# Routing attention and an MLP mixer on one core: six chunks of scores in one run, then six of values

## The chip, the core and the metric

The kernel runs on one core of one Trainium2 chip. The metric is the device time of one execution in microseconds (us). Three runs of the kernel before gave 885.87, 886.28 and 886.34 us; the median is 886.28. The profile shown is of one further execution, whose run took 886.28 us, and whose first and last profiled instructions lie 884.2 us apart: that distance is called the span below.

## What is computed

There are 4 batches and 8 heads, each with 768 queries, 768 keys and values of depth 64. Every query and key is assigned to the centroid it is most similar to (16 per head), and a query attends only to the keys with its own centroid. The outputs of the heads, side by side, are the 768 x 512 input of a mixer.

```python
q_assign = np.argmax(np.einsum('bhsd,hcd->bhsc', q_n, c_n), axis=-1)
k_assign = np.argmax(np.einsum('bhsd,hcd->bhsc', k_n, c_n), axis=-1)
scores = scale * np.matmul(q, k.transpose(0, 1, 3, 2))
scores = np.where(q_assign[..., :, None] == k_assign[..., None, :], scores, -1e9)
attn = softmax(scores)
x = (attn @ v), heads side by side
h = np.maximum(x.transpose(0, 2, 1) @ w_tok1, 0.0) @ w_tok2
u = x + h.transpose(0, 2, 1)
out = u + np.maximum(u @ w_ch1, 0.0) @ w_ch2
```

## The kernel before, in words

**Pairs and chunks.** The attention handles two heads at a time: 16 pairs g (4 batches x 4), one after the other. The 768 keys are six chunks of 128 (`NJ = 6`), the 768 queries two halves `qh` of 384 (`HS`). One chunk for one half of the queries is the smallest piece of work: 12 of them in a pair, 192 in all. The scores of a chunk lie with the keys on the partitions, and for both heads, in one tile `sc` of 2 x 512 fp32[...]. The pool `ps_sc` has three such tiles.

- **Scores (L430).** For each of the two heads a bf16 matmul of the one-hot rows of the centroids (`ohT`), which gives a large negative number wherever the centroids differ, and then a fp32 matmul of keys and queries (`T`, shown as `qkT`). The heads lie on partitions 0 to 63 and 64 to 127, so each matmul uses 64 rows of the array. A fp32 matmul is two instructions in the trace.
- **Exponential (L436).** ScalarE (ACT) turns one `sc` tile into a tile `ex` of 128 x 768, of which there are six (pool `work`).
- **Values (L461).** For each head `va` times `ex`, into 64 columns of the array, summed over the six chunks in the one tile `av`; ACT copies it to `avT` (L469).
- **Sums (L447, L451).** VectorE (DVE) adds the six `ex` of a half up. This gives the denominators.

**Small steps of a pair.** `load(g)` (L132) issues nine DMAs on SyncE's queue (SP). `turn(g)` (L284) transposes the queries and keys on DVE in blocks. `route_products` (L298) multiplies them with the centroids; `route` (L308), `route_big` (L337) and `route_count` (L330, on ACT) find the centroids and mark them; `route_turn` (L339) transposes the marks with a DMA. `pair_sums` (L478), `pair_denominators` (L482) and `pair_reciprocals` (L485) treat the denominators of the pair before, `half_turn` (L491) transposes its `avT`, and `half_out` (L499) divides and stores. Two tiles named `small` and `px`, for L298, L478 and L491, come from the same three tiles of `ps_sc`.

**Rounding of the weights.** `weight_steps` (L177) loads pieces of the mixer's weights and rounds them: per step three DVE operations, two ACT operations and a DMA. There are two steps in each of the first six pairs (`EARLY`), then one.

**Order.** The order on each engine is the order in which the code issues, since the kernel is built with a manual schedule. L816 loops over groups `m` of three chunks, four groups to a pair. In each turn it issues the sums of group m-1, the scores of group m and the values of group m-1: values follow one group late. The small steps hang on `s`, the group's number within its pair. `scores` issues the bf16 matmuls of two chunks, the fp32 ones of these two, and then those of the third chunk.

**Begin and end.** `begin` (L764) handles pair 0 apart: `turn_first` (L367) transposes on TensorE into a tile `pt`, whose two halves (queries, keys) are copied out by ACT (L790) and DVE (L791); L793 (ACT) and L279 (DVE) copy the centroids out of `pc`; L395 (ACT) and L393 (DVE) copy the marks out of `po`. After the last group come the token products (`tok1` L526, `tok2` L537), in their midst the small steps of the last pair (L857), and then the channel products, 525 us of the span.

Of the kernel before, what the change touches and what calls it, by code (L numbers as in the profile page):

```python
# [8 lines left out]
F32 = mybir.dt.float32  # L9
# [3 lines left out]
ALU = mybir.AluOpType  # L13
ACT = mybir.ActivationFunctionType
AX = mybir.AxisListType

B, H, S, D = 4, 8, 768, 64
C = 16
P = 128
NJ = S // P  # L20
DM = H * D
# [9 lines left out]
QP = P // NQ  # L31
NPAIR = B * NF

NG = 3
GROUPS = 2 * NJ // NG
EARLY = 6
SM_SCALE = 0.125

# [9 lines left out]
def kernel(  # L48
# [35 lines left out]
    def pool(name, bufs, stack=None, **kw):  # L84
        return (stack or fast).enter_context(
            tc.tile_pool(name=name, bufs=bufs, reuse_waits="tile", **kw)
        )
# [1 line left out]
    ps_w = pool("ps_w", 1, space=PSUM)  # L89
    ps_av = pool("ps_av", 1, space=PSUM)  # L90
    ps_sc_stack = fast.enter_context(ExitStack())
    ps_sc = pool("ps_sc", NG, ps_sc_stack, space=PSUM)

    xpool = pool("xpool", 1)
    wc1pool = pool("wc1pool", 1)
# [268 lines left out]
                    )  # L364
        nc.sync.dma_start(st["va"], v[0, 0:2].rearrange("h (p j) d -> p h j d", p=P))

    def turn_first(n):  # L367
        st = state[0]
        pt = ps_sc.tile([P, 2, 512], F32, tag="sc", name="pt")
        js = slice(HJ * n, HJ * n + HJ)  # L370
        for a in (1, 0):
            for j in range(HJ):
                nc.tensor.transpose(
                    out=pt[:, a, j * P : (j + 1) * P],
                    in_=st["rows"][:, n, a, j].rearrange("p h d -> p (h d)"), identity=ident,
                )
        return [
            (st["T"][:, a, js].rearrange("p j t -> p (j t)"), pt[:, a, 0:HS]) for a in range(2)
        ]

    def route_turn_first(n):
        po = ps_w.tile([P, 2, HJ, P], BF16, tag="w", name="po")
# [7 lines left out]
    def route_first_out(n, po, a):  # L390
        out = state[0]["ohT"][:, a, HJ * n : HJ * n + HJ]
        if a == 0:
            nc.vector.tensor_scalar_mul(out=out, in0=po[:, 0], scalar1=-BIG)  # L393
        elif n == 0:
            nc.scalar.copy(out=out, in_=po[:, 1])  # L395
        else:
            nc.vector.tensor_copy(out=out, in_=po[:, 1])

    def second_first():

        po = route_turn_first(1)
        for a in (1, 0):
            route_first_out(1, po, a)
        for n in range(2):
            route_count(0, slice(HJ * n, HJ * n + HJ), NPAIR * n)
        nc.vector.tensor_tensor(
            out=cells[:, 0:1], in0=cells[:, 0:1], in1=cells[:, NPAIR : NPAIR + 1], op=ALU.add
        )
        state[0].pop("rows")


    def split(m):

        g, s = divmod(m, GROUPS)
        return g, s // (GROUPS // 2), NG * (s % (GROUPS // 2))

    def scores(m):
        g, qh, j0 = split(m)
        st = state[g]
        js = slice(HJ * qh, HJ * qh + HJ)  # L420
        scs = [ps_sc.tile([P, 2, 512], F32, tag="sc", name="sc") for _ in range(NG)]

        for chunks in (range(NG - 1), (NG - 1,)):
            if m == 0 and len(chunks) == 1:
                second_first()
            for src, start in ((st["ohT"], True), (st["T"], False)):
                for i in chunks:
                    for h in range(2):
                        rows = slice(h * D, (h + 1) * D)
                        nc.tensor.matmul(  # L430
                            scs[i][:, h, 0:HS], lhsT=src[rows, 1, j0 + i], rhs=src[rows, 0, js],
                            start=start, stop=not start,
                        )
        for i in range(NG):
            ex = work.tile([P, 2, HS], F32, name="ex")
            nc.scalar.activation(out=ex, in_=scs[i][:, :, 0:HS], func=ACT.Exp, scale=SM_SCALE)  # L436
            st["ex", qh, j0 + i] = ex

    def add_up(m):
        g, qh, j0 = split(m)  # L440
        st = state[g]
        e = [st["ex", qh, j0 + i] for i in range(NG)]
        if j0 == 0:
            if qh == 0:
                st["sum"] = sums.tile([P, 2, 2, HS], F32, name="sum")
            acc = st["sum"][:, qh]
            nc.vector.tensor_tensor(out=acc, in0=e[0], in1=e[1], op=ALU.add)  # L447
            e = e[2:]
        acc = st["sum"][:, qh]
        for ex in e:  # L450
            nc.vector.tensor_tensor(out=acc, in0=acc, in1=ex, op=ALU.add)  # L451

    def values(m):
        g, qh, j0 = split(m)
        st = state[g]
        if j0 == 0:
            st["av"] = ps_av.tile([P, HS], F32, name="av")
        for j in range(j0, j0 + NG):
            ex = st.pop(("ex", qh, j))
            for h in range(2):  # L460
                nc.tensor.matmul(  # L461
                    st["av"][h * D : (h + 1) * D], lhsT=st["va"][:, h, j], rhs=ex[:, h],
                    start=(j == 0), stop=(j == NJ - 1),
                )
        if j0 == NJ - NG:
            if qh == 0:
                st["avT"] = sums.tile([P, NJ, P], F32, name="avT")
            js = slice(HJ * qh, HJ * qh + HJ)
            nc.scalar.copy(out=st["avT"][:, js].rearrange("p j t -> p (j t)"), in_=st.pop("av"))  # L469

    def pair_sums(g, den):

# [291 lines left out]
    def begin():  # L764
# [21 lines left out]
        keep_warm(12)  # L786
        pc = centroids_norm(cen)
        keep_warm(2)
        tq, tk = turn_first(0)
        nc.scalar.copy(out=tq[0], in_=tq[1])  # L790
        nc.vector.tensor_copy(out=tk[0], in_=tk[1])  # L791
        centroids_out(pc)
        nc.scalar.copy(out=cnT, in_=pc)  # L793
        keep_warm(2)
        pr = ps_sc.tile([P, 2, 512], F32, tag="sc", name="pr")
        route_products(0, pr[:, 0, 0 : HS // 2], js[0])
        for out, src in turn_first(1):
            nc.scalar.copy(out=out, in_=src)
        route(0, js[0])
        keep_warm(2)  # L800
        po = route_turn_first(0)
        for a in (1, 0):
            route_first_out(0, po, a)
# [2 lines left out]

    begin()
    weights = list(weight_steps(stage, W, ("tok1", "tok2", "ch1")))
    last = NPAIR * GROUPS
    ends = [lambda t=t: tok1(0, t) for t in range(NT)]  # L810
    for b in range(B):
        if b + 1 < B:
            ends += [lambda b=b, t=t: tok1(b + 1, t) for t in range(NT)]
        ends += [lambda b=b, j=j: tok2(b, j) for j in range(NJ)]

    for m in range(last + 3):  # L816
        g, s = divmod(m, GROUPS)
        more = g < NPAIR - 1
        old = g - 1 if m < last else -1
        if s == 2:  # L820
            if old >= 0:
                pair_denominators(old)
            if more:
                route(g + 1)
                route_big(g + 1)
                route_count(g + 1)
            if old >= 0:
                pair_reciprocals(old)
        if s == 3 and old >= 0:
            for qh in range(2):  # L830
                half_out(old, qh)
        if more and s == 0 and m > 0:
            turn(g + 1)
        if 1 <= m <= last:
            add_up(m - 1)
        if m < last:
            scores(m)
        if m == 0:
            turn(1)
        if 1 <= m <= last:  # L840
            values(m - 1)
        if m < last and s == 1:
            two = ps_sc.tile([P, 2, 512], F32, tag="sc", name="small")
            if old >= 0:
                pair_sums(old, two[:, 0, 0:HS])
            if more:
                route_products(g + 1, two[:, 1, 0:HS])
        if more and s == 2:
            route_turn(g + 1)
        if m < last and s == 2 and old >= 0:  # L850
            two = ps_sc.tile([P, 2, 512], F32, tag="sc", name="px")
            for qh in range(2):
                half_turn(old, qh, two[:, qh, 0:HS])
        if m == last:
            ps_sc_stack.close()
            pools["ps_m"] = pool("ps_m", 2, space=PSUM)
        if m == last + 1:  # L857
            pair_sums(NPAIR - 1, ps_w.tile([P, HS], F32, tag="w", name="den"))
            pair_denominators(NPAIR - 1)
            pair_reciprocals(NPAIR - 1)  # L860
            half_turn(NPAIR - 1, 0, ps_w.tile([P, HS], F32, tag="w", name="px"))
            half_turn(NPAIR - 1, 1, ps_av.tile([P, HS], F32, name="av"))
        if m == last + 2:
            for qh in range(2):
                half_out(NPAIR - 1, qh)
        if s == 1 and g + 2 < NPAIR:
            load(g + 2)
        if m == last - GROUPS:
            assert not weights
            routing.close()  # L870
            W["ch2"] = pool("wc2pool", 1, side="right").tile([P, NCT, DM], F32, name="wc2")
            weights = list(weight_steps(stage, W, ("ch2",)))
        if m < last - GROUPS:

            n = s == 1 or s == 3 and g < EARLY
        else:
            n = m % 2 if m < last else 2
        for _ in range(min(n, len(weights))):
            weights.pop(0)()
        if m >= last:  # L880
            for _ in range(3):
                ends.pop(0)()
    assert not state
    attention.close()
    pools["wsums"] = pool("wsums", 1, side="right")
# [239 lines left out]
```

## Time and profile before

| engine | busy us | share of the span | what it does most |
|---|---|---|---|
| PE (TensorE, matmuls) | 869.9 | 98% | L430, L461, later L662 and L713 |
| PEld (TensorE, loads of the stationary operand) | 519.0 | 59% | beside PE |
| DVE (VectorE) | 492.1 | 56% | L451 |
| ACT (ScalarE) | 289.3 | 33% | L436 |
| POOL (GpSimd) | 42.2 | 5% | rounding |

The DMA engines are busy for 22.6% of the span on the main queue. The clock granted to TensorE is 0.997 of full speed on the mean. A row of a group says: line, engine, operation, output and inputs, shapes and count, then busy time in us and the mean duration of one in ns, then how long the engine was idle ahead of the group and who ended that. A row of the timeline says: start in us, time until the last of the merged instructions ends, engine, line, operation and count. "PE busy" counts to a modelled end of each matmul, so that two matmuls in a row overlap in the record, and a pause shorter than that overlap isn't seen as idle.

### The profile page before, as it was taken

The page shows a single profiled execution, that of the slowest core. Times are in us where ns is not written, and L with a number is a line of the kernel's source. Part 1 is how long each engine was busy: PE and PEld are TensorE (multiplying, and loading weights), DVE is VectorE, ACT ScalarE, POOL GpSimd, SP SyncE. Part 2 cuts the span into 40 slices and gives each one's busy share as a digit, 9 for nine tenths or more (in the row PEclk, how much of TensorE's full clock was granted, in tenths as well). Part 3 has the DMA queues.
Part 4 walks back from the last instruction along what each step waited for, and adds up shares of the span by engine and source line. Part 5 has one row for each costly group of instructions (what it writes and reads, how often), then busy time and mean ns, then how long its engine had stood idle before and what let it go on. Part 6 is the DMA issues. An engine that isn't in the chain of part 4 may idle for free.

```text
span 884.2 us, 11022 instructions
## 1 busy us (share of the span) xinstructions
PE 869.9 (98%) x4293; PEld 519.0 (59%) x4293; DVE 492.1 (56%) x847; ACT 289.3 (33%) x507; POOL 42.2 (5%) x40
## 2 busy tenths in 40 slices
PE   8999999999999999999999999999999999999996
PEld 4444444444444444444568587686776867768675
DVE  5788888777777765695463334433344333343342
ACT  3665665555555454221120311203113021120210
POOL 1010011000010001230000000000000000000000
PEclk9999999999999999999999999999999999999998
DMA  8655665444554121220000001000010000100001
GB/s 159 148 121 118 140 131 112 100 96 97 106 120 80 19 91 47 85 82 1 0 1 1 0 29 44 0 1 1 24 48 1 0 1 25 47 1 1 0 25 50
DMA packets 133275, 47.61 MB, mean 54 GB/s; under 512 B 122080, under 2 KB 126176, under 8 KB 133216
## 3 DMA queue, kind: packets, MB, share of 16 engines
q1 hardware_dynamic: 131616, 46.45, 22.6%
q8 instruction: 35, 0.57, 0.3%
q10 hardware_dynamic: 1600, 0.39, 0.2%
q14 instruction: 24, 0.20, 0.1%
HBM read 34.64 MB, written 6.29 MB: 46 GB/s over the span
## 4 chain that ended last, share of the span: by engine, by line
PE 97%; DVE 1%; ACT 1%; DMA 0%; issue 0%; DVEq 0%
PE sc L430 18%; PE av L461 15%; PE pX L713 14%; PE pX L662 14%; PE pZ L713 7%; PE pZ L662 7%; PE ph L531 5%; PE pu L540 5%; PE pY L713 4%; PE pY L662 4%; PE px L491 1%; PE small L478 1%; PE pt L603 1%; PE small L298 1%; ACT uT L606 0%; DMA cen<-in_centroids_dram 0%
## 5 line engine op out<-in xcount | busy, mean ns | idle before, releaser
L436 ACT ACTIVATE ex<-sc 128x768 f32<-128x768 f32 x192 | 143.8, 807 | 63.3 <-PE sc L430 46.8
L430 PE MATMUL sc<-qkT 64*128 64x384 f32 x768 | 144.7, 482 | 0.0
L461 PE MATMUL av<-ex,va 128*64 128x384 f32 x768 | 137.8, 494 | 0.0
L451 DVE TENSOR_TENSOR sum<-sum,ex 128x768 f32<-128x768 f32 x128 | 121.1, 946 | 10.6 <-DVE sum L447 0.5
L461 PEld LDWEIGHTS av<-ex,va 128*64 128x64 f32 x768 | 49.5, 136 | 80.5 <-issue 63.2
L430 PEld LDWEIGHTS sc<-qkT 64*128 64x128 f32 x768 | 69.6, 187 | 35.1 <-issue 14.1
L662 PE MATMUL pX<-uT,wc 128*128 128x384 f32 x192 | 67.4, 487 | 0.0
L670 ACT COPY p<-pX 128x384 f32<-128x384 f32 x24 | 11.4, 475 | 148.1 <-PE pX L662 148.1
L430 PE MATMUL sc<-ohT 64*128 64x384 bf16 x384 | 52.8, 326 | 0.4 <-DVE ohT L393 0.4
L662 PEld LDWEIGHTS pX<-uT,wc 128*128 128x128 f32 x192 | 36.2, 190 | 24.7 <-issue 1.0
L223 POOL TENSOR_TENSOR wc<-wT,wup 128x512 int32<-128x512 int32 x24 | 30.7, 1278 | 262.1 <-DVE wT L216 262.1
L540 PE MATMUL pu<-h,wt 128*128 128x512 f32 x96 | 42.0, 592 | 0.0
L531 PE MATMUL ph<-x,wt 128*128 128x512 f32 x96 | 42.0, 593 | 0.0
L557 DVE TENSOR_TENSOR c<-pZ,u 128x384 f32<-128x384 f32 x24 | 13.4, 557 | 46.9 <-PE pZ L662 46.9
L482 DVE STREAM_TRANSPOSE dent<-small 128x384 f32<-128x384 f32 x15 | 8.7, 583 | 54.8 <-PE small L298 49.4
L557 DVE TENSOR_TENSOR x<-pX,x 128x256 f32<-128x256 f32 x24 | 10.2, 423 | 49.3 <-PE pX L713 49.3
L430 PEld LDWEIGHTS <-ohT 64*128 64x128 bf16 x384 | 13.6, 94 | 40.6 <-issue 31.5
L557 DVE TENSOR_TENSOR hA<-pY,p 128x384 f32<-128x384 f32 x24 | 13.4, 557 | 40.1 <-PE pY L662 40.1
L713 PE MATMUL pX<-w2s,hA 128*128 128x256 f32 x144 | 35.1, 380 | 0.5 <-DVE x L557 0.5
L713 PE MATMUL pX<-wc,hA 128*128 128x256 f32 x144 | 35.0, 379 | 0.0
L713 PE MATMUL pY<-wc,hA 128*128 128x256 f32 x144 | 35.0, 379 | 0.0
L713 PE MATMUL pZ<-w2s,hS 128*128 128x256 f32 x144 | 35.0, 379 | 0.0
(130 smaller groups left out, 1196.1 us busy)
## 6 DMA issues: line engine op xcount, KB each, us to landing
raw<-in_moe_w_ch_dram SPq DMA_DIRECT2D x24, 512.0 KB, 4.1
qk<-in_k_dram SPq DMA_DIRECT2D x64, 96.0 KB, 4.1
va<-in_v_dram SPq DMA_DIRECT2D x16, 384.0 KB, 3.4
out_dram<-x SPq DMA_DIRECT2D x24, 256.0 KB, 2.0
qk<-in_q_dram SPq DMA_DIRECT2D x60, 96.0 KB, 3.5
raw<-in_moe_w_tok_dram SPq DMA_DIRECT2D x3, 512.0 KB, 4.9
raw<-in_moe_w_tok_dram SPq DMA_DIRECT2D x4, 384.0 KB, 4.1
qk<-in_q_dram ACTq DMA_DIRECT2D x4, 96.0 KB, 3.3
```

The costliest lines, as they stand in the source:

```text
L223: nc.gpsimd.tensor_tensor(out=dst.bitcast(I32), in0=T, in1=up, op=ALU.add)
L298: nc.tensor.matmul(pr[rows], lhsT=cnd[:, f].rearrange("p i c -> p (i c)"), rhs=st["T"][:, :, js, rows], start=True, stop=True,)
L430: nc.tensor.matmul(scs[i][:, h, 0:HS], lhsT=src[rows, 1, j0 + i], rhs=src[rows, 0, js], start=start, stop=not start,)
L436: nc.scalar.activation(out=ex, in_=scs[i][:, :, 0:HS], func=ACT.Exp, scale=SM_SCALE)
L451: nc.vector.tensor_tensor(out=acc, in0=acc, in1=ex, op=ALU.add)
L461: nc.tensor.matmul(st["av"][h * D : (h + 1) * D], lhsT=st["va"][:, h, j], rhs=ex[:, h], start=(j == 0), stop=(j == NJ - 1),)
L531: nc.tensor.matmul(pf, lhsT=W["tok1"][:, j, t * P : (t + 1) * P], rhs=xs[b][:, j], start=(j == 0), stop=(j == NJ - 1),)
L540: nc.tensor.matmul(pu, lhsT=W["tok2"][:, t, j], rhs=h1s[b][:, t], start=(t == 0), stop=(t == NT - 1))
L557: nc.vector.tensor_tensor(out=dst, in0=a, in1=b, op=ALU.add)
L662: nc.tensor.matmul(psum, lhsT=A[a][:, k, c * P : (c + 1) * P], rhs=R[r][:, k], start=start and k == 0, stop=k == 1, skip_group_check=not s ...
L670: nc.scalar.copy(out=kept[name], in_=psum)
L713: nc.tensor.matmul(psum, lhsT=h2[a][:, k, i * P : (i + 1) * P], rhs=Bw[w][:, 3 * part + k], start=start and k == 0, stop=k == 2, skip_grou ...
```

## The change

The loop over groups of three chunks is replaced by a loop over pairs. In a pair, the six chunks of the first half of the queries are scored in one run, and the six values follow at once, with no lag of a group; then the second half in the same way. The steps on TensorE that are neither go to two places: the denominators of the pair before and the routing of the next one behind the first values, the transposes of the pair before behind the second ones. `scores` issues each chunk's bf16 and fp32 matmuls together, followed by its exponential. `load(g + 2)` goes to the start of pair g, `turn` one pair ahead (`turn(g + 2)` in the second half of pair g, after the sums), `route_turn` right behind `route_big`, `route_count` behind the exponentials of the second half, `half_out` to the pair's end, and the rounding steps behind the first sums and at the pair's end. In `begin` the transposes of queries and keys go to two tiles, the centroids are copied out ahead of them, both marks are copied by DVE, and one idle matmul is added. At the end, the denominators of the last pair come ahead of the first `tok1`, and its transposes and `half_out` behind that. The number of tiles in each pool stays the same.

```diff
-    def turn_first(n):
+    def turn_first(n, tiles):
...
-        elif n == 0:
-            nc.scalar.copy(out=out, in_=po[:, 1])
         else:
             nc.vector.tensor_copy(out=out, in_=po[:, 1])
...
-        for chunks in (range(NG - 1), (NG - 1,)):
-            if m == 0 and len(chunks) == 1:
+        for j in range(NJ):
+            if (g, qh, j) == (0, 0, 2):
                 second_first()
+            sc = ps_sc.tile([P, 2, 512], F32, tag="sc", name="sc")
             for src, start in ((st["ohT"], True), (st["T"], False)):
-                for i in chunks:
-                    for h in range(2):
...
+                for h in range(2):
+                    rows = slice(h * D, (h + 1) * D)
+                    nc.tensor.matmul(
+                        sc[:, h, 0:HS], lhsT=src[rows, 1, j], rhs=src[rows, 0, js],
+                        start=start, stop=not start,
+                    )
+            ex = st["ex", j] = work.tile([P, 2, HS], F32, name="ex")
+            nc.scalar.activation(out=ex, in_=sc[:, :, 0:HS], func=ACT.Exp, scale=SM_SCALE)
...
+        scs = [ps_sc.tile([P, 2, 512], F32, tag="sc", name="pt") for _ in range(2)]
+        centroids_out(pc)
+        nc.scalar.copy(out=cnT, in_=pc)
+        tq, tk = turn_first(0, [x[:, 0, 0:HS] for x in scs])
         nc.scalar.copy(out=tq[0], in_=tq[1])
         nc.vector.tensor_copy(out=tk[0], in_=tk[1])
-        centroids_out(pc)
-        nc.scalar.copy(out=cnT, in_=pc)
...
-        keep_warm(2)
+        keep_warm(3)
         po = route_turn_first(0)
...
-    for m in range(last + 3):
...
+    for g in range(NPAIR):
+        more, old, final = g < NPAIR - 1, g - 1, g == NPAIR - 1
+        if g + 2 < NPAIR:
+            load(g + 2)
...
+        scores(g, 0)
+        if g == 0:
+            turn(1)
+        add_up(g, 0)
+        rounding(1)
+        values(g, 0)
+        if more or old >= 0:
+            two = ps_sc.tile([P, 2, 512], F32, tag="sc", name="small")
+            if old >= 0:
+                pair_sums(old, two[:, 0, 0:HS])
+            if more:
+                route_products(g + 1, two[:, 1, 0:HS])
             if old >= 0:
                 pair_denominators(old)
             if more:
                 route(g + 1)
                 route_big(g + 1)
-                route_count(g + 1)
+                route_turn(g + 1)
             if old >= 0:
                 pair_reciprocals(old)
...
+        scores(g, 1)
+        if more:
+            route_count(g + 1)
+        add_up(g, 1)
+        if g + 2 < NPAIR:
+            turn(g + 2)
+        values(g, 1)
+        if old >= 0:
             two = ps_sc.tile([P, 2, 512], F32, tag="sc", name="px")
             for qh in range(2):
                 half_turn(old, qh, two[:, qh, 0:HS])
...
+            for qh in range(2):
+                half_out(old, qh)
+        rounding(g < EARLY or final)
+
+    pair_sums(NPAIR - 1, ps_w.tile([P, HS], F32, tag="w", name="den"))
+    pair_denominators(NPAIR - 1)
+    pair_reciprocals(NPAIR - 1)
+    ps_sc_stack.close()
+    pools["ps_m"] = pool("ps_m", 2, space=PSUM)
+    for m in range(9):
+        ends.pop(0)()
+        if m == 0:
             half_turn(NPAIR - 1, 0, ps_w.tile([P, HS], F32, tag="w", name="px"))
             half_turn(NPAIR - 1, 1, ps_av.tile([P, HS], F32, name="av"))
...
+            for qh in range(2):
+                half_out(NPAIR - 1, qh)
+        if m % 3 == 2:
+            rounding(2)
```

More of the change, by code (lines that the diff above doesn't have):

```diff
@@ L32 @@
 NPAIR = B * NF
-NG = 3
-GROUPS = 2 * NJ // NG
 EARLY = 6
@@ L91 @@
     ps_sc_stack = fast.enter_context(ExitStack())
-    ps_sc = pool("ps_sc", NG, ps_sc_stack, space=PSUM)
+    ps_sc = pool("ps_sc", 3, ps_sc_stack, space=PSUM)
     xpool = pool("xpool", 1)
@@ L365, in load_first @@
         nc.sync.dma_start(st["va"], v[0, 0:2].rearrange("h (p j) d -> p h j d", p=P))
-    def turn_first(n):
+    def turn_first(n, tiles):
         st = state[0]
-        pt = ps_sc.tile([P, 2, 512], F32, tag="sc", name="pt")
         js = slice(HJ * n, HJ * n + HJ)
@@ L373, in turn_first @@
                 nc.tensor.transpose(
-                    out=pt[:, a, j * P : (j + 1) * P],
+                    out=tiles[a][:, j * P : (j + 1) * P],
                     in_=st["rows"][:, n, a, j].rearrange("p h d -> p (h d)"), identity=ident,
                 )
-        return [
-            (st["T"][:, a, js].rearrange("p j t -> p (j t)"), pt[:, a, 0:HS]) for a in range(2)
-        ]
+        return [(st["T"][:, a, js].rearrange("p j t -> p (j t)"), tiles[a]) for a in range(2)]
     def route_turn_first(n):
@@ L409, in second_first, with scores @@
         state[0].pop("rows")
[L412 to L418, printed above, removed]
+    def scores(g, qh):
         st = state[g]
         js = slice(HJ * qh, HJ * qh + HJ)
-        scs = [ps_sc.tile([P, 2, 512], F32, tag="sc", name="sc") for _ in range(NG)]
-        for chunks in (range(NG - 1), (NG - 1,)):
-            if m == 0 and len(chunks) == 1:
+        for j in range(NJ):
+            if (g, qh, j) == (0, 0, 2):
@@ L425, in scores @@
                 second_first()
+            sc = ps_sc.tile([P, 2, 512], F32, tag="sc", name="sc")
             for src, start in ((st["ohT"], True), (st["T"], False)):
-                for i in chunks:
-                    for h in range(2):
[L429 to L440, printed above, removed]
-        st = state[g]
[L442 to L448, printed above, removed]
-        acc = st["sum"][:, qh]
-        for ex in e:
-            nc.vector.tensor_tensor(out=acc, in0=acc, in1=ex, op=ALU.add)
@@ L453, in values @@
-    def values(m):
-        g, qh, j0 = split(m)
+                for h in range(2):
[6 more added lines that the diff above has]
+            nc.scalar.activation(out=ex, in_=sc[:, :, 0:HS], func=ACT.Exp, scale=SM_SCALE)
@@ L455, in values, with add_up @@
+    def add_up(g, qh):
+        st = state[g]
+        if qh == 0:
+            st["sum"] = sums.tile([P, 2, 2, HS], F32, name="sum")
+        acc = st["sum"][:, qh]
+        for j in range(1, NJ):
+            nc.vector.tensor_tensor(
+                out=acc, in0=acc if j > 1 else st["ex", 0], in1=st["ex", j], op=ALU.add
+            )
+    def values(g, qh):
         st = state[g]
[L456 to L459, printed above, removed]
+        av = ps_av.tile([P, HS], F32, name="av")
+        for j in range(NJ):
+            ex = st.pop(("ex", j))
@@ L460, in values @@
             for h in range(2):
                 nc.tensor.matmul(
-                    st["av"][h * D : (h + 1) * D], lhsT=st["va"][:, h, j], rhs=ex[:, h],
+                    av[h * D : (h + 1) * D], lhsT=st["va"][:, h, j], rhs=ex[:, h],
                     start=(j == 0), stop=(j == NJ - 1),
                 )
[L465 to L469, printed above, removed]
+        if qh == 0:
+            st["avT"] = sums.tile([P, NJ, P], F32, name="avT")
@@ L471, in pair_sums @@
+        js = slice(HJ * qh, HJ * qh + HJ)
+        nc.scalar.copy(out=st["avT"][:, js].rearrange("p j t -> p (j t)"), in_=av)
     def pair_sums(g, den):
@@ L788, in begin @@
         keep_warm(2)
-        tq, tk = turn_first(0)
+        scs = [ps_sc.tile([P, 2, 512], F32, tag="sc", name="pt") for _ in range(2)]
+        centroids_out(pc)
+        nc.scalar.copy(out=cnT, in_=pc)
+        tq, tk = turn_first(0, [x[:, 0, 0:HS] for x in scs])
         nc.scalar.copy(out=tq[0], in_=tq[1])
         nc.vector.tensor_copy(out=tk[0], in_=tk[1])
-        centroids_out(pc)
-        nc.scalar.copy(out=cnT, in_=pc)
         keep_warm(2)
@@ L796, in begin @@
         route_products(0, pr[:, 0, 0 : HS // 2], js[0])
-        for out, src in turn_first(1):
+        pt = ps_sc.tile([P, 2, 512], F32, tag="sc", name="pt")
+        for out, src in turn_first(1, [pt[:, a, 0:HS] for a in range(2)]):
             nc.scalar.copy(out=out, in_=src)
         route(0, js[0])
-        keep_warm(2)
+        keep_warm(3)
         po = route_turn_first(0)
@@ L808 @@
     weights = list(weight_steps(stage, W, ("tok1", "tok2", "ch1")))
-    last = NPAIR * GROUPS
     ends = [lambda t=t: tok1(0, t) for t in range(NT)]
@@ L814, with rounding @@
         ends += [lambda b=b, j=j: tok2(b, j) for j in range(NJ)]
-    for m in range(last + 3):
[L817 to L820, printed above, removed]
+    def rounding(n):
+        for _ in range(min(n, len(weights))):
+            weights.pop(0)()
+    for g in range(NPAIR):
+        more, old, final = g < NPAIR - 1, g - 1, g == NPAIR - 1
+        if g + 2 < NPAIR:
+            load(g + 2)
+        if final:
+            assert not weights
+            routing.close()
+            W["ch2"] = pool("wc2pool", 1, side="right").tile([P, NCT, DM], F32, name="wc2")
+            weights = list(weight_steps(stage, W, ("ch2",)))
+        scores(g, 0)
[10 more added lines that the diff above has]
+                route_products(g + 1, two[:, 1, 0:HS])
             if old >= 0:
@@ L825 @@
                 route_big(g + 1)
-                route_count(g + 1)
+                route_turn(g + 1)
             if old >= 0:
                 pair_reciprocals(old)
[L829 to L850, printed above, removed]
+        scores(g, 1)
[6 more added lines that the diff above has]
+        if old >= 0:
             two = ps_sc.tile([P, 2, 512], F32, tag="sc", name="px")
@@ L853 @@
                 half_turn(old, qh, two[:, qh, 0:HS])
[L854 to L860, printed above, removed]
+            for qh in range(2):
[9 more added lines that the diff above has]
+        if m == 0:
             half_turn(NPAIR - 1, 0, ps_w.tile([P, HS], F32, tag="w", name="px"))
             half_turn(NPAIR - 1, 1, ps_av.tile([P, HS], F32, name="av"))
-        if m == last + 2:
             for qh in range(2):
                 half_out(NPAIR - 1, qh)
[L866 to L882, printed above, removed]
+        if m % 3 == 2:
+            rounding(2)
     assert not state
```

## The prediction

> **What bounds the kernel.** I read the engine shares first, then the chain that ended last, then the waits, then the timeline of one pair.
>
> ```profile
> PE 869.9 (98%) x4293; PEld 519.0 (59%) x4293; DVE 492.1 (56%) x847; ACT 289.3 (33%) x507; POOL 42.2 (5%) x40
> ...
> PE 97%; DVE 1%; ACT 1%; DMA 0%; issue 0%; DVEq 0%
> ```
>
> TensorE is the chain. But a busy share of 98% doesn't say that it works at its peak, so I turn to the starts of its instructions. The timeline of pair 7, rows of PE and what feeds it:
>
> ```profile
> 151.47 2.16 PE L461 MATMUL av<-ex,va 128*64 128x384 f32 x12
> ...
> 152.49 0.14 PEld L461 LDWEIGHTS av<-ex,va 128*64 128x64 f32 x2 [0.18 <-issue]
> 152.81 0.14 PEld L461 LDWEIGHTS av<-ex,va 128*64 128x64 f32 x2 [0.18 <-issue]
> ...
> 153.56 0.50 PE L430 MATMUL sc<-ohT 64*128 64x384 bf16 x4
> ...
> 153.89 1.45 PE L430 MATMUL sc<-qkT 64*128 64x384 f32 x8
> ...
> 155.18 0.33 PE L430 MATMUL sc<-ohT 64*128 64x384 bf16 x2
> ...
> 155.34 0.81 PE L430 MATMUL sc<-qkT 64*128 64x384 f32 x4
> ...
> 156.08 2.16 PE L461 MATMUL av<-ex,va 128*64 128x384 f32 x12
> ...
> 168.82 0.88 PE L491 MATMUL px<-ident,avT 128*128 128x128 f32 x6
> ...
> 169.63 0.50 PE L430 MATMUL sc<-ohT 64*128 64x384 bf16 x4
> ...
> 172.16 2.16 PE L461 MATMUL av<-ex,va 128*64 128x384 f32 x12
> ```
>
> The reader is to see beats. Two heads run side by side, so instructions go in twos: a beat of values or fp32 scores is 0.32 us (152.49 to 152.81; 153.89 to 155.18 is four beats), one of bf16 scores 0.16 (155.18 to 155.34). A group of three chunks therefore needs 6 x 0.322 = 1.93 for values and 3 x (0.16 + 2 x 0.322) = 2.41 for scores, 4.35 in all. It takes 4.61 (151.47 to 156.08). The missing **0.26 us** is no wait for data, since it returns in every group. It lies where the kind of matmul changes: single starts give 0.144 from scores to values, 0.113 from values to scores. A pair takes 20.69 (151.47 to 172.16): four groups (18.44), the two products in `small` (1.43), `px` (0.81). By the starts of `px` all pairs from 1 to 14 have this length.
>
> **The Trainium skill.** TensorEngine Tiling (Array Packing), Key Properties, says that changing the tiling mode drains the engine. Scores use tiles of 64x128, values 128x64, and the trace shows 0.26 for each round trip. Perfetto Trace Analysis, Per-engine timelines, says that a matmul's end in the profile is estimated; that is why these pauses appear as busy, and it agrees with the 482 ns records on a 0.32 beat. PSUM — Partial Sum Buffer, on bank collisions, asks for order between engines on one bank. Here even the halves of `pt`, in two banks, are read one after the other: L791 on DVE waits 1.98 until ACT's L790 has read the same tile. L793 waits for L279, which shares only its source `pc`.
>
> **Step 1, fewer changes of mode.** Before there are 63 changes from scores to values (64 groups, the last two values join), after it 32: 31 x 0.144 = 4.5. Direct changes from values to scores fall by 31 too (two in each pair; the two with small products between them remain): 31 x 0.113 = 3.5. Sum **-8.0**; a middle pair falls from 20.69 to 20.15. Chunk by chunk order of bf16 and fp32 costs nothing: the third chunk (155.18 to 155.34) already runs so with full beats, and its weight loads lie under matmuls.
>
> **Step 2, the end.** Now the stretch is: last values, 0.416 to `ph`, 0.523 from `ph` to `den`, 1.194 from `den` to `px` (DVE's L482 comes late, PE idle for 0.7). After it: `px` of pair 14 to `den` 0.205 (this replaces `px` to scores), `den` to `ph` 0.418, `ph` to `px` 0.523; the DVE work (rounding 1.68, L482 and L485 0.8) hides under the first `ph`, 5.16. 2.13 - 0.94 = **-1.2**.
>
> **Step 3, the begin.** With two tiles DVE's copy needn't wait for ACT's, and the centroids (0.45) run ahead of it: the first products start when ACT's copy ends (7.44) and not at 8.54, if source tiles are what orders the copies. Then both marks on DVE take 0.63 in place of 0.86 from ACT's start to DVE's end (10.88 to 11.74): 0.2 more. The further idle matmul (0.16) lies under DVE's routing. If the common destination `qkT` orders them instead, 0.45 + 0.2 remain. I take **-1.1**, bounds -1.3 and 0.
>
> **Step 4, the rings.** Three `sc` tiles, runs of six: chunk j+3 waits for exponential j. A chunk is 0.805 on PE, so chunk 3 wants to start at 2.42 after the run's start S. The first exponential starts 0.49 + 0.54 = 1.03 after S (last matmul's start, then what the trace shows from there to ACT), takes 0.81, and PE starts 0.05 after an ACT release (L603): 1.89. Slack 0.5. ACT keeps pace: 2.26 for three is one per 0.73. What stands ahead on ACT: `avT` starts 0.53 after the last value beat, takes 0.48; with `px` on PE it is over 0.2 before S. In pairs 1 to 5 two rounding operations (1.24) follow it, until S + 1.0: just in time. Only the way from pair 0 to 1 has no `px`: ACT is free at S + 1.8, 0.8 late, less 0.5 slack: **+0.3**. Values of chunk 5 want their exponential at 8.2, it ends at 5.9. The six `ex` are free (sums end at 7.9, next use 11.4).
>
> **Step 5, what moves on DVE and SP.** Second half, from its run's start S1: L482 at 0.13, routing and reciprocals until 2.8, five sums at 1.01 until 7.8, `turn` 1.91 (two of 0.95) until 9.8; the next run starts at S1 + 9.77. `half_out` can start 0.25 after that start, so DVE is just free; it takes 1.02 and ends at 1.27. The third chunk takes `px`'s tile at 1.61: slack 0.3. `small`: readers end 1.18 after S1, wanted at 1.61. In the first half rounding (1.68, in pairs 1 to 5 twice) and sums end at 9.7, ahead of L482 at 10.5. Busy DVE is 17.3 in an early pair, of 20.15. Cost 0; upper bound below. SP: nine DMAs of `load(g+2)` are issued by some 1.2 after the pair's start and land 4.1 later; `turn(g+2)` asks at 18. `route_turn` is issued at 13.0 and lands 3.8 later (5.2 at most), wanted at 20.15. Behind it on SP stand a weight piece, wanted 7 us or more later, and the next load. `route_count` (0.5 on ACT) goes behind the exponentials, where ACT has 3 us free. The number of rounding steps before the last pair stays 21; `tok1` follows with full tiles.
>
> **Sum.** -8.0 - 1.2 - 1.1 + 0.3 = -10.0 against the span of 884.2: 874.2. The runs' time stands 2.1 above the span, and the profiled run is the median: **876.3**. The channel products, 525 us, I leave as they are: neither code nor data change.
>
> **Rivals.**
> - Forecast (chance 0.78): 876.3, own range 875.0 to 878.0. For it: the 0.26 returns with every group, whatever ACT and DVE do.
> - The change at the begin doesn't do what it says (0.10): destination or another tile orders the copies, and DVE is late with the first routing: 877.4. Against it: the wait of L793.
> - The score ring paces the runs (0.06). If ACT starts 0.8 late in each of 32 runs, chunk 3 waits 0.3 each time: 9.6, and with -10.0 it is no change: 885.9. For it: today three tiles serve three chunks, and no run is longer. Against it: 0.5 slack by the rows above.
> - DVE holds `px` (0.06), slower. The third chunk after `px` waits for `half_out`, behind sums and `turn`. DVE decides from the point where `half_out` ends later than 1.56 after the run's start; each us beyond is lost on PE in 15 pairs. Were the sums or the landing for `turn` 1.3 us later, 1.0 would be lost per pair: 15 - 10 = +5, 891. Against it: DVE is idle for 2.8 of 20.15 us in an early pair, 4.3 in a later one, and the sums start with the second exponential.
>
> Range 874.5 to 880.0: it takes the begin's bounds and some tenths of ring waits in the early pairs; beyond it lie the last two rivals. A change of 0.2% (1.8 us) is about what a measurement can tell from none. Faster 0.91, same 0.03, slower 0.06.
>
> **What would show it.** Right: pairs of 20.15, with two changes from scores to values in each in place of four, and 0.26 for each round trip as before; L430's first start near 10.7; no wait of `px` on L482. Wrong: PE idle ahead of the third chunk of a run (released by L499 or L314) would show the DVE rival, ahead of the fourth (released by L436) the ring; longer beats in the six-chunk runs would mean that the alternation of bf16 and fp32 isn't free.

## The result, and the profile after

The changed kernel takes 877.77 us (median of six runs, 877.49 to 878.35), against 886.17 in the runs of the kernel before beside it: a ratio of 0.9906 with a 95% interval from 0.9893 to 0.9919, 8.4 us less. The prediction was 876.3. The span of the profiled execution is 875.5, against 884.2.

The page of the changed kernel, engine shares and then the chain that ended last:

```profile
PE 862.4 (99%) x4294; PEld 522.8 (60%) x4294; DVE 504.9 (58%) x848; ACT 297.8 (34%) x506; POOL 44.2 (5%) x40
...
PE 95%; DVE 3%; ACT 1%; issue 0%; DVEq 0%
```

TensorE (PE) is still the chain, but VectorE (DVE) now holds 3% of it in place of 1%. That is a first sign that DVE has come into the way somewhere. Where, the waits of PE between 330 and 400 us show (who waited for whom: us in total, times, longest):

```profile
PE ph L508 <- DVE x L520: 0.7, 1, 0.7
PE ph L508 <- DVE x L476: 0.4, 1, 0.4
```

Both are new; in the kernel before, PE waited once in this place, for the denominators of the last pair:

```profile
PE px L491 <- DVE dent L482: 0.7, 1, 0.7
```

The attention itself looks as it was drawn. The timeline of the second half of pair 6, PE's matmuls alone:

```profile
140.27 0.83 PE L296 MATMUL small<-qkT,cnd 128*32 128x384 f32 x8
141.03 0.34 PE L416 MATMUL sc<-ohT 64*128 64x384 bf16 x2
141.20 0.81 PE L416 MATMUL sc<-qkT 64*128 64x384 f32 x4
141.85 0.33 PE L416 MATMUL sc<-ohT 64*128 64x384 bf16 x2
...
145.24 0.81 PE L416 MATMUL sc<-qkT 64*128 64x384 f32 x4
145.98 4.09 PE L439 MATMUL av<-ex,va 128*64 128x384 f32 x24
150.00 0.88 PE L468 MATMUL px<-ident,avT 128*128 128x128 f32 x6
150.81 0.34 PE L416 MATMUL sc<-ohT 64*128 64x384 bf16 x2
```

A chunk of scores follows the other every 0.81 us (141.03, 141.85), six of them fill 141.03 to 145.98, and the values follow without a wait for data. The next pair's scores start at 150.81. By the starts of `px` every pair from 2 to 14 takes 20.18, against 20.69 before.

By stretches of PE's timeline, before and after:

| stretch | before | after | difference |
|---|---|---|---|
| start to the first score matmul | 11.80 | 10.14 | -1.66 |
| from there to the first `pu` (tok2) | 352.35 | 344.25 | -8.10 |
| from there to the first `pX` | 65.46 | 66.47 | +1.01 |
| from there to the end | 454.58 | 454.60 | +0.02 |
| span | 884.2 | 875.5 | -8.7 |

### The profile page after: what moved, and what is told of

The parts are those of the page before. It is cut to its first block, busy times and chain, and to the rows that moved or that the text cites. A ratio compares the mean times of both kernels' runs of the same rounds, so it can differ in the third digit from the quotient of the medians.

```text
span 875.5 us, 11022 instructions
## 1 busy us (share of the span) xinstructions
PE 862.4 (99%) x4294; PEld 522.8 (60%) x4294; DVE 504.9 (58%) x848; ACT 297.8 (34%) x506; POOL 44.2 (5%) x40
## 4 chain that ended last, share of the span: by engine, by line
PE 95%; DVE 3%; ACT 1%; issue 0%; DVEq 0%
PE sc L416 18%; PE av L439 15%; PE pX L690 14%; PE pX L639 14%; PE pZ L690 7%; PE pZ L639 7%; PE ph L508 4%; PE pY L690 4%; PE pY L639 4%; PE pu L517 3%; PE px L468 1%; PE small L455 1%; PE pt L580 1%; PE small L296 1%; DVE wh L209 1%; DVE wT L214 1%
## 5 line engine op out<-in xcount | busy, mean ns | idle before, releaser
L421 ACT ACTIVATE ex<-sc 128x768 f32<-128x768 f32 x192 | 152.6, 811 | 44.8 <-PE sc L416 42.6
L416 PE MATMUL sc<-qkT 64*128 64x384 f32 x768 | 155.1, 482 | 0.0
L429 DVE TENSOR_TENSOR sum<-sum,ex 128x768 f32<-128x768 f32 x128 | 125.3, 979 | 13.7 <-ACT ex L421 0.5
L439 PE MATMUL av<-ex,va 128*64 128x384 f32 x768 | 130.9, 490 | 0.0
L439 PEld LDWEIGHTS av<-ex,va 128*64 128x64 f32 x768 | 52.2, 137 | 74.8 <-issue 71.0
L416 PE MATMUL sc<-ohT 64*128 64x384 bf16 x384 | 63.0, 324 | 0.3 <-DVE ohT L389 0.2
L429 DVE TENSOR_TENSOR sum<-ex 128x768 f32<-128x768 f32 x32 | 32.0, 1001 | 20.3 <-ACT ex L421 20.2
L446 ACT COPY avT<-av 128x384 f32<-128x384 f32 x32 | 15.3, 479 | 83.1 <-PE av L439 83.1
L416 PEld LDWEIGHTS <-ohT 64*128 64x128 bf16 x384 | 19.2, 94 | 35.4 <-issue 13.6
```

The costliest lines, as they stand in the source:

```text
L416: nc.tensor.matmul(sc[:, h, 0:HS], lhsT=src[rows, 1, j], rhs=src[rows, 0, js], start=start, stop=not start,)
L421: nc.scalar.activation(out=ex, in_=sc[:, :, 0:HS], func=ACT.Exp, scale=SM_SCALE)
L429: nc.vector.tensor_tensor(out=acc, in0=acc if j > 1 else st["ex", 0], in1=st["ex", j], op=ALU.add)
L439: nc.tensor.matmul(av[h * D : (h + 1) * D], lhsT=st["va"][:, h, j], rhs=ex[:, h], start=(j == 0), stop=(j == NJ - 1),)
```

## The experiments

Eight variants of the changed kernel, and that kernel once more. Four of them (two score tiles, two chunks at a time, `half_out` behind the rounding step, one tile for the first transposes) were executed once; what they show is read from their traces. The theory is that of the prediction: PE sets the pace, each change of the kind of matmul costs it a fixed price, and the rings of buffers behind it are just deep enough. The rivals are named with each run.

**One more round trip in each run.** Scores of four chunks, values of two, scores of two, values of four.

```diff
-        scores(g, 0)
+        scores(g, 0, range(4))
+        values(g, 0, range(2))
+        scores(g, 0, range(4, NJ))
...
-        values(g, 0)
+        values(g, 0, range(2, NJ))
```

> The changed kernel, but each run of six is cut once: scores of four chunks, values of two, scores of two, values of four. Same instructions, 32 more changes from scores to values and 32 more back. Theory (a change of the kind of matmul costs 0.144 and 0.113 us): 32 x 0.257 = 8.2 us more span, 875.5 to 883.7, and a middle pair of 20.18 + 0.51 = 20.69. Rival (the gain came from the lag of a group being gone, or from the order of ACT and DVE): span within 1 us of 875.5, pairs of 20.2.

Measured: 886.41 us against 886.14 of the kernel before, ratio 1.0001 (0.9992 to 1.0009). The whole gain is gone. The span is 884.4: 8.9 above the changed kernel's, of which 0.54 came before the first score matmul (10.68 against 10.14). From there to the first `pu` it takes 352.50 in place of 344.25: 8.25, where 8.2 was expected. The timeline of the second half of pair 6 in this kernel:

```profile
144.94 0.34 PE L416 MATMUL sc<-ohT 64*128 64x384 bf16 x2
...
147.53 0.81 PE L416 MATMUL sc<-qkT 64*128 64x384 f32 x4
148.27 1.51 PE L441 MATMUL av<-ex,va 128*64 128x384 f32 x8
149.72 0.34 PE L416 MATMUL sc<-ohT 64*128 64x384 bf16 x2
...
151.43 2.80 PE L441 MATMUL av<-ex,va 128*64 128x384 f32 x16
154.16 0.88 PE L472 MATMUL px<-ident,avT 128*128 128x128 f32 x6
154.97 0.34 PE L416 MATMUL sc<-ohT 64*128 64x384 bf16 x2
```

From its first scores to those of the next pair this half takes 10.03 (144.94 to 154.97), in the changed kernel 9.78 (141.03 to 150.81). By the starts of `px` pairs 2 to 14 take 20.69 each, to the hundredth what they took in the kernel before, though the lag of a group is gone, the small products lie in their new places and ACT and DVE work in the new order. So the gain of the attention is the number of changes, 0.257 us for each round trip.

**Two score tiles in place of three.** The edit is the number in `pool("ps_sc", 3, ...)`.

> The changed kernel with two score tiles in place of three. Theory (chunk j+2 must wait for exponential j, which ends 1.89 us after the chunk's start, where PE would want it at 1.61): 0.28 for every second chunk, 0.56 per run, 18 us in 32 runs, and the second chunk after small and px waits for DVE's readers, 0.4 to 0.5 each, 15 us in all: span about 875.5 + 33 = 908, slower than the kernel before. Rival (the ring is slack, three tiles are more than a run needs): span below 880.

Measured: span 907.5, 909.62 us. The waits of PE in this kernel:

```profile
PE sc L416 <- ACT ex L421: 6.5, 30, 0.9
PE sc L416 <- DVE sim L312: 3.6, 14, 0.3
PE sc L416 <- DVE x L476: 2.9, 14, 0.2
```

All three releasers that the expectation named are there: the exponentials, and the readers of `small` and `px`. The totals in this view are small (13 us of 32), because PE's records run on to a modelled end: a wait shows as idle only where it outlasts that. The starts give the true cost: a pair takes 22.2 in place of 20.18, 2.02 more, where 2.05 was worked out. The ring of three is no luxury; two would make the change a loss.

**Two chunks at a time.** Scores of a run in twos: bf16 of both chunks, then fp32 of both.

```diff
-        for j in range(NJ):
+        for j0 in range(0, NJ, 2):
...
+            scs = [ps_sc.tile([P, 2, 512], F32, tag="sc", name="sc") for _ in range(2)]
             for src, start in ((st["ohT"], True), (st["T"], False)):
-                for h in range(2):
+                for i in range(2):
+                    for h in range(2):
```

> The changed kernel, but the scores of a run go two chunks at a time, as before: bf16 of both, then fp32 of both. Same instructions, same number of changes of kind. Theory (order within a run decides whether three tiles suffice): the first chunk of two is ready 0.16 later and the second tile is asked for 0.64 earlier, so the second chunk of the second and third two waits about 0.28 for its exponential: 0.55 per run, 17.6 in 32 runs, span about 893. Rival (order within a run is free, 0.5 us of slack cover it): span 875 to 877.

Measured: span 894.3, 896.38 us, slower than the kernel before. A pair takes 21.28, 1.10 more than 20.18: 0.55 per run, as expected. The timeline of one run:

```profile
140.20 0.77 PE L417 MATMUL sc<-ohT 64*128 64x384 bf16 x4
...
140.79 1.47 PE L417 MATMUL sc<-qkT 64*128 64x384 f32 x8
141.65 1.51 ACT L423 ACTIVATE ex<-sc 128x768 f32<-128x768 f32 x2 [0.36 <-PE sc L417]
142.08 0.77 PE L417 MATMUL sc<-ohT 64*128 64x384 bf16 x4
```

Four bf16 matmuls take 0.59 (140.20 to 140.79) where two beats of 0.16 would do; the second two wait 0.27 for an exponential. Of these waits, 17.6 us in all, the list of waits shows 0.8: a record runs 0.16 past its beat, so only 0.1 of each shows as idle time, which is too short for that list. Placing each chunk's bf16 and fp32 together was thus a condition of the change, not a detail of it.

**half_out behind the rounding step.**

```diff
-            for qh in range(2):
-                half_out(old, qh)
         rounding(g < EARLY or final)
+        if old >= 0:
+            for qh in range(2):
+                half_out(old, qh)
```

> The changed kernel, with half_out put behind the rounding step at a pair's end. Only pairs 1 to 5 have DVE work in that step. Theory (px's tile is wanted 1.61 us after the next run's start and is free at 1.3, so DVE may be 0.3 late): rounding of 1.7 (512 wide, three pairs) or 1.3 (384 wide, two pairs) ahead of half_out costs PE 1.3 and 1.0 per pair, 5.9 us in all, span 881.4, with PE waiting on half_out's line ahead of the third chunk. Rival (DVE's margin is wider, or the pool takes another tile): span within 1 us of 875.5.

Measured: span 880.8, 882.96 us. PE's waits:

```profile
PE sc L416 <- DVE x L476: 3.6, 5, 1.0
```

Five waits, behind the five pairs. The starts of `px` give 21.04, 20.78, 21.13, 21.04 and 21.33 for the pairs that follow them and 20.18 for the others: 4.4 us in all, not 5.9. The mechanism of the slower rival is real and sits where it was put. Its price was a quarter lower, for two reasons. In four of the five places the rounding step starts 0.27 before the point at which `half_out` starts in the changed kernel, since it needn't wait for `px`. And `half_out` ends there 1.13 after the run's start, not 1.3, while the third chunk starts at 1.62: its end moves by 1.03 to 1.58 in this kernel, and the third chunk by 0.43 less each time.

**The begin undone.** In the second set the changed kernel ran again as its measure (`after_again`: 877.95 us, ratio to the kernel before 0.9906, span 875.7).

> The changed kernel itself, as the measure for the three others of this set: about 877.8, span 875.5, first score matmul 4.9 us after the transpose of the centroids.

```diff
-        scs = [ps_sc.tile([P, 2, 512], F32, tag="sc", name="pt") for _ in range(2)]
-        centroids_out(pc)
-        nc.scalar.copy(out=cnT, in_=pc)
+        pt = ps_sc.tile([P, 2, 512], F32, tag="sc", name="pt")
...
         nc.vector.tensor_copy(out=tk[0], in_=tk[1])
+        centroids_out(pc)
+        nc.scalar.copy(out=cnT, in_=pc)
```

The mark copied by ACT and the idle matmul are undone too.

> The changed kernel with the begin of the kernel before (one tile for both transposes, centroids copied out behind them, one mark copied by ACT, one idle matmul fewer). Theory (copies from one source tile on two engines are put one after the other, and the centroids stand in the path): the first score matmul starts 6.15 us after the transpose of the centroids in place of 4.9, and the time is 1.3 higher. Rival (the earlier start in the changed kernel came from an earlier landing of the centroids, 0.4 of 1.66, and the rest from the first pair's new order): difference below 0.4.

Measured: 878.8 us, 0.85 more, interval of the ratio 0.9901 to 0.9928, which overlaps the other's; the traces decide. From the transpose of the centroids to the first score matmul it takes 6.16 in place of 4.88: 1.28, the theory's figure. (Counted from the first transpose of queries and keys it is 5.69 in place of 4.41, the same 1.28; this count leaves out how early the data landed.) But 0.49 comes back later. The end of the attention here, then in the changed kernel:

```profile
333.29 0.85 PE L457 MATMUL den<-sum,ones 128*32 128x384 f32 x8
334.07 5.42 PE L510 MATMUL ph<-x,wt 128*128 128x512 f32 x12
```

```profile
331.78 0.85 PE L455 MATMUL den<-sum,ones 128*32 128x384 f32 x8
333.06 5.39 PE L508 MATMUL ph<-x,wt 128*128 128x512 f32 x12 [0.42 <-DVE x L476]
```

From `den` to the first `ph` it is 0.78 here and 1.28 in the changed kernel; counted from the last `den` matmul, as the prediction counts, 0.416 and 0.909. The old begin takes one score tile fewer from the ring of three, so at the end `px` of pair 14 should lie in another tile than the one whose bank the first token product wants; the traces show the wait and its releaser, not the addresses. 1.28 - 0.49 = 0.79.

**One tile for the first transposes, nothing else undone.** The edit is the first line of the diff above.

> The changed kernel, with the first transposes of queries and keys in one tile again and nothing else undone. Theory (copies out of one tile by two engines are put one after the other): DVE's copy of the keys starts when ACT's of the queries has ended, 0.55 after that the first centroid products, so that the first score matmul starts 5.4 us after the transpose of the centroids in place of 4.88. Rival (the earlier centroids and the marks on one engine make the whole 1.28): 4.88 as in the changed kernel.

Measured: from the transpose of the centroids to the first score matmul 5.47, 0.59 more (span 875.9). The timeline of this kernel, then that of the changed one:

```profile
6.86 0.48 ACT L770 COPY qkT<-pt 128x384 f32<-128x384 f32 x1 [0.16 <-PE pt L371]
7.37 0.56 DVE L771 COPY qkT<-pt 128x384 f32<-128x384 f32 x1 [1.03 <-ACT qkT L770]
7.98 0.53 PE L296 MATMUL pr<-qkT,cnd 128*32 128x192 f32 x8 [0.83 <-DVE qkT L771]
```

```profile
6.26 0.56 DVE L771 COPY qkT<-pt 128x384 f32<-128x384 f32 x1 [0.20 <-PE pt L371]
6.38 0.49 PE L760 MATMUL av<-warm 128*128 128x384 bf16 x2
6.58 0.48 ACT L770 COPY qkT<-pt 128x384 f32<-128x384 f32 x1 [0.16 <-PE pt L371]
7.12 0.53 PE L296 MATMUL pr<-qkT,cnd 128*32 128x192 f32 x8 [0.24 <-ACT qkT L770]
```

With one source tile the two copies stand in a row; with two they overlap, though both write `qkT`. It is the source, and it is worth 0.59 of the 1.28. The order is written into the program: DVE's copy waits here for the semaphore of ACT's copy (a wait of 1.03, released by L770), in the changed kernel for TensorE's alone. The other 0.69 is the earlier centroids and the marks on one engine; these two weren't parted. This kernel, too, takes one score tile fewer at the begin, and from `den` to `ph` it shows 0.416 again: so most of the 0.59 comes back, and the time, 877.98 us, is that of the changed kernel.

**The rounding beside the token products ahead of each three, as before.**

```diff
     for m in range(9):
+        if m % 3 == 0:
+            rounding(2)
         ends.pop(0)()
...
-        if m % 3 == 2:
-            rounding(2)
```

> The changed kernel, but the rounding steps beside the token products come ahead of each three of them, as in the kernel before, and not behind. Theory (the steps came 15 us later against TensorE, so that DVE's sums of the token products ran late and PE waited 0.75 for L520): the wait goes, and with it 0.9 of the time. Rival (DVE is the bound of that stretch in any case, the wait only moves): span as in the changed kernel, with a wait at another place.

Measured: 876.91 us against 877.95, span 874.7. The wait for L520 is gone; of the two new waits this one is left:

```profile
PE ph L508 <- DVE x L476: 0.4, 1, 0.4
```

From the first `pu` to the first `pX` it takes 65.45, as in the kernel before, where `after_again` takes 66.48: 1.0 in place of the 0.9 expected. DVE's share of the chain that ended last falls from 3% to 0%.

**Both ends mended.** As the last one, and in the last pair `half_turn` and `half_out` of pair 14 come behind `pair_reciprocals`, in the first half.

> As early_rounding, and in the last pair the transposes of the pair before come behind the first values, beside its denominators, so that the first token product finds its bank free. Theory: the wait of 0.42 for half_out goes, 0.5 less than early_rounding, 1.4 less than the changed kernel: about 876.4. Rival: the third chunk of the last run then waits for px, and the gain is below 0.2.

Measured: 876.17 us, ratio to the kernel before 0.9884 (0.9869 to 0.9899), the fastest of all: the slowest of its four runs took 876.24, the fastest of `early_rounding` 876.69. The changed kernel beside it had a ratio of 0.9906 (0.9891 to 0.9921). From `den` to `ph` it is 0.416 again, and the third chunk of the last run doesn't wait.

## Why the prediction was right

**Step 1, the changes of kind (-8.0): right.** The traces count 63 changes from scores to values before and 32 after, and `one_more_trip` puts 32 round trips back and gets the same pair, 20.69. A middle pair was to be 20.15 and is 20.18; here the forecast had slipped, for 20.69 less two round trips of 0.257 is 20.18.

**Step 2, the end (-1.2): right about the wait, and mis-sized: it brought 0.4.** The wait of `px` on L482 went, as written. But "`den` to `ph` 0.418" was wrong: it is 0.909. The token products' banks are those of the score tiles, and the first one waits for `half_out` of pair 14 (L476), which had to read `px`. Which of the three tiles that is depends on how many had been taken in all: the two begins with one tile fewer, `old_begin` and `shared_pt`, show the 0.416 that was forecast, and every other kernel here with this end shows 0.91. And the sum takes the 0.416 from the last values to `ph` as saved in full. Of it 0.32 is the last beat of the values, which is work in any order, and the 0.1 of the change is already among the 31 of step 1: only 30 of the direct changes from values to scores went (31 before, one after), and this is the 31st. The other way, `ph` to `px` took 0.43 in place of 0.52.

**A move that was left out (+1.0).** "`tok1` follows with full tiles" and "the number of rounding steps before the last pair stays" passed over those beside the token products. They came from ahead of each three of them to behind, some 15 us on PE. There DVE has two things to do for each `pu`, the sum that releases its bank (L520) and a rounding step, 2.9 us together against 1.72 of PE, so it falls behind, and a later start is paid at the end. `early_rounding` shows that. The prediction counted the steps and not their place. (Of the 2.9 us, 0.76 is lost beside GpSimd: L204 takes 1.18 there and 0.42 elsewhere.)

**Step 3, the begin (-1.1): right in mechanism, 1.28 in size,** inside its bounds. What would have remained if the destination ordered the copies, 0.65, agrees with the 0.69 that `shared_pt` leaves. The stretch shows 1.66 because the centroids landed 0.38 earlier in this execution (2.44 against 2.82); that is luck, and no gain of the change: over the runs shown here the transpose of the centroids starts between 5.26 and 5.67.

**Step 4, the rings: right but for its one cost.** The 0.5 us of slack stood the test: it is what `two_sc` and `two_by_two` go beyond, by amounts that the same walk gives. The +0.3 on the way from pair 0 to 1 was to come from ACT being 0.8 late; that run takes 4.58 in place of 4.54, so ACT costs 0.04. Instead the run before it takes 4.82: its third chunk waits 0.27 for the exponential of the run's first.

```profile
21.26 0.33 PE L416 MATMUL sc<-ohT 64*128 64x384 bf16 x2
21.47 1.62 ACT L421 ACTIVATE ex<-sc 128x768 f32<-128x768 f32 x2 [1.22 <-PE sc L416]
22.33 0.34 PE L416 MATMUL sc<-ohT 64*128 64x384 bf16 x2
```

By that wait, the pool gave out the first chunk's tile and not that of `small`, so this run had two tiles to turn over. Why the pool chose so stays open. The size agrees with the forecast by luck, at another place.

**Step 5, DVE and SP (0): right for the pairs.** Its margins were there and a little wider (`half_out` ends at 1.13, not 1.27), and `late_half_out` shows what lies beyond them.

Sum after the first score matmul up to `pu`: forecast -8.0 - 1.2 + 0.3 = -8.9, measured -8.1: 0.4 for the 0.416 counted as saved in full, 0.5 at the bank, -0.1 in the step from `ph` to `px`. With the rounding (+1.0) and the begin (-0.6 against the forecast, 0.4 of it luck) the span comes out 1.3 above the 874.2 foreseen. So the main term was right in mechanism and size, while three misses of 0.4, 0.5 and 1.0 at the end of the attention and a lucky begin lie in the rest; the range was wide enough for them, but had been drawn for other things. Of the rivals none took place; that of the ring and that of DVE each describe a kernel that could be built, 1.10 and 0.88 us per pair away.

## What to carry to other kernels

Where TensorE is busy for 98% of the time, count the starts and not the busy share: a price that returns with every change of the shape of its tiles stands in no list of waits, and longer runs of one kind are the way to pay it less often. Before making runs longer, walk the ring of buffers once around (chunk start, end of its reader, start of the chunk that takes the same buffer), since a run pays each missing tenth of a microsecond in every repetition. And when steps are moved, price each one at the place where it lands: an equal number of them is no argument.

## What the runs showed of the hardware

The price of a change is the same in the kernel before, the changed one and `one_more_trip`: 0.412 us from the start of the last score instruction to that of the first values, where the beat would be 0.32, with a slower first step of values after it (0.37), and 0.418 the other way. It goes with the shape of the tile, not with the type or with another target: from the fp32 scores of one chunk to the bf16 scores of the next, into another tile of PSUM, it is 0.319, the plain beat. The runs show this price; what the engine does in that time they don't show. A wait shorter than the difference between a fp32 matmul's record (482 ns) and its beat (320 ns) doesn't show as idle time of PE in these traces, and a longer one shows shorter by as much: 0.27 as 0.1 in `two_by_two`.

The Trainium skill (SBUF — State Buffer, Who interferes with whom) says that a DVE instruction with two inputs in SBUF contends with a GpSimd instruction that reads SBUF, and the trace agrees. The timeline of the changed kernel:

```profile
133.37 0.96 DVE L429 TENSOR_TENSOR sum<-ex 128x768 f32<-128x768 f32 x1
133.49 1.97 POOL L221 TENSOR_TENSOR wc<-wT,wup 128x512 int32<-128x512 int32 x1 [11.21 <-DVE wT L214]
134.43 5.03 DVE L429 TENSOR_TENSOR sum<-sum,ex 128x768 f32<-128x768 f32 x4
...
141.19 1.27 POOL L221 TENSOR_TENSOR wc<-wT,wup 128x512 int32<-128x512 int32 x1 [5.73 <-DVE wT L214]
...
144.83 4.15 DVE L429 TENSOR_TENSOR sum<-sum,ex 128x768 f32<-128x768 f32 x4
```

With a sum of two SBUF tiles beside it the GpSimd addition takes 1.97 in place of 1.27, and four sums take 5.03 in place of 4.15. The new order brings the two together at five places, behind pairs 1 to 5, and takes 0.7 to 0.9 us of DVE's time at each. In the kernel before, the same addition ran beside `turn` (L288), which has one input, and took 1.27 to 1.28 there. PE doesn't feel it: the pairs behind those five take 20.18 like the others.
